# Split w_out for the second slot's second product of a linear-attention and FFN kernel

## The chip, the cores and the metric

The kernel runs on one core of one Trainium2 chip. The metric is the device time of one execution in microseconds; lower is better. Three runs of the kernel before took 598.08, 599.2 and 603.07 us (median 599.2).

## What is computed

Two steps: a causal linear attention with a complex decay per channel, and behind it a feed-forward network (FFN) whose activation is a rational function.

```python
mag = np.sqrt(a_re * a_re + a_im * a_im)
scale = np.minimum(mag, 0.999) / (mag + 1e-06)
a_re_n, a_im_n = (a_re * scale, a_im * scale)
for t in range(S):                       # S = 768; B, H, D = 4, 8, 48
    new_re = ar * S_re - ai * S_im       # ar, ai: a_re_n, a_im_n at t
    new_im = ar * S_im + ai * S_re
    S_re, S_im = (new_re + kv, new_im)   # kv: outer product of k and v at t
    y[:, :, t] = np.einsum('bhd,bhde->bhe', q[:, :, t], S_re)
...
x = y.transpose(0, 2, 1, 3).reshape(B * S, H * D)    # 3072 x 384
h = x @ w_in                                         # 384 x 2048
P = a[0] + a[1] * h + a[2] * h2 + a[3] * h3
Q = 1.0 + np.abs(b[0]) * np.abs(h) + np.abs(b[1]) * h2
g = P / (Q + 1e-06)
return g @ w_out                                     # 2048 x 384
```

q, k, v and the decays are float32; w_in and w_out come as float64.

## The kernel before

**Units and slots.** The sequence is cut into 6 chunks of 128 steps. A unit is one chunk of one batch (24 units); two units make a pair, and the kernel works through 12 pairs, its slots. For a unit, `norm` and `angle` build the decay's running product `MM` (three scans) and its running angle `T` (one scan for two units), `trig` takes sines and arc tangents on ScalarE (ACT), `outer` multiplies q and k by them into `Q`, and DMAs turn the result over into `HQ`. `attn` then does the matmuls on TensorE (PE): keys turned (L611), scores (L624), which VectorE (DVE) masks into `ST`, values (L642), and the chunk's contribution to the state `St` (L662). x of the unit is written to a ring of three.

**The FFN of a slot** is `ffn` (L678). The first four slots take one pair each, 256 tokens; after that, two pairs go together, 512 tokens. h is made 128 of its 2048 rows at a time, a block; there are 16 blocks f, and in the first four slots two blocks share a bank `ph` and make a group, 8 groups to a slot. A group goes through these steps: first product into `ph` (L701, PE); on ACT squares, an absolute value and a reciprocal square root (L366) in the buffers `Af` and `Zf`; on DVE the operations that join them to g (L351); second product (L717, PE), which adds the group's two blocks to the sums in `po0` and `po1`. The second product of a group is written behind the first product of the group two further on. There are four buffers g, three `Af`, two `Zf` and three banks `ph`.

**Split and unsplit.** Matmuls are done in one of two ways. Unsplit, both operands are float32: one matmul for each of the three 128-wide strips of the 384 columns. Split, weight and moving operand are each a high half in the type fp32r and a low half (the rest), and three matmuls high x high, low x high, high x low stand for one, nine for a block. The global `WHOLE = 2` says that slots 0 and 1 use unsplit weights, for both products; later slots use split ones. With unsplit weights ACT's second square root step lies in a PSUM bank (`po2`), and DVE has four operations for a group: `ph`, `Af<-Af,co,po`, `Af<-Af,po`, `g<-ph,co,Af`. With split weights g is made as two halves and there are five: `ph`, `g<-ph,co,Zf` (the high half), `Af<-Af,co,g`, `Af<-ph,co,Af`, and the low half `g<-Af,Zf`, which can run on DVE or GpSimd (POOL).

**Weights.** w_in and w_out arrive as raw float64 bits by DMA and are folded to float32 tiles `wi` (12 of 128 x 512) and `wo` (16 of 128 x 384) by `fold` (L431 to L449). `split` then makes the halves of all weights, with `halve`: the high half is a copy (L465 when ACT does it), the low half a subtraction (L351) on DVE or POOL. High halves of w_out are called `wh`, its low halves take the tile of a `wo` that is used up. L1041 to L1044 place all of it around the end of slot 1, in the order's time from 1.3 to 2.5 slots.

**What sets the order.** Operations are collected in a plan, each with the engines that could run it. The global `ORDER` (L235) is a recorded table: the position of each operation in the program and its engine. Instructions of one engine run in that order. DMAs are issued from SyncE (SP), save a few from ACT. `rouse` (L667, L673) adds matmuls into an unused bank (fillers, `po<-wi,ident` and `po<-Q,ident`, 128 x 256 each, two records), which the order may put on PE or drop.

## Time and profile before

| | |
|---|---|
| median of three runs | 599.2 us |
| profiled execution | 602.15 us, span 600.5 us |
| mean granted clock of TensorE | 0.973 |
| busy share of PE, DVE, ACT, POOL | 93%, 91%, 87%, 47% |
| stretch 0 to 57 us | loads, folding, the first two units |
| 57 to 112 us, 112 to 168 us | FFN of slots 0 and 1, both unsplit |
| 168 to 214 us, 214 to 270 us | FFN of slots 2 and 3, split, 256 columns |
| from 270 us on | wide FFN slots, 512 columns |

The profile is one execution, seen by the hardware profiler. The stretches are where the first products of a slot begin, within some us, since neighbouring slots overlap. A busy PE is not PE at its peak, since matmuls are pipelined and their ends are modelled. A float32 matmul that is not split shows as two records. The idle time of an instruction is what its engine idled ahead of it, with the instruction that ended the wait as the trace infers it.

### The profile page before, as it was taken

What the parts mean: (1) busy time and instruction counts of PE and PEld (TensorE: products, weight loads), DVE (VectorE), ACT (ScalarE), POOL (GpSimd) and SP (SyncE); (2) the same over time, 40 slices, a digit from 0 to 9 for tenths busy, and PEclk for the clock granted to TensorE, in tenths of its full rate; (3) what the DMA queues carried; (4) which work ended last, traced back from release to release, by engine and by line L of the source; (5) the groups of instructions that cost most, each with busy time, mean ns of one, the idle gap of its engine ahead of it and who ended that gap; (6) DMA issues with size and microseconds to landing.
All of it is one profiled execution on the core that took longest, in us unless ns stands there. A gap on an engine that the chain in (4) does not pass through costs nothing.

```text
span 600.5 us, 15652 instructions
## 1 busy us (share of the span) xinstructions
PE 558.3 (93%) x6240; PEld 470.2 (78%) x6240; DVE 543.7 (91%) x924; ACT 524.7 (87%) x872; POOL 284.3 (47%) x253
## 2 busy tenths in 40 slices
PE   0467999999999999999999999999999999999995
PEld 0356888888899998997888788878888887878884
DVE  7996999899999999999999989999898788889884
ACT  7986999999998999989999989979998796588781
POOL 4483555357554648536674753555615346000000
PEclk9766999999999999999999999999999999999998
DMA  8996466464532365546362145324053314110001
GB/s 298 292 262 213 141 139 140 116 150 96 100 107 49 79 157 130 103 119 134 90 128 71 41 117 136 101 37 137 28 121 112 47 36 100 21 52 2 0 2 58
DMA packets 39185, 64.02 MB, mean 107 GB/s; under 512 B 4416, under 2 KB 25152, under 8 KB 39104
## 3 DMA queue, kind: packets, MB, share of 16 engines
q1 hardware_dynamic: 38528, 62.28, 41.4%
q8 instruction: 51, 0.84, 0.7%
q10 hardware_dynamic: 576, 0.66, 0.5%
q14 instruction: 30, 0.25, 0.1%
HBM read 39.32 MB, written 4.72 MB: 73 GB/s over the span
## 4 chain that ended last, share of the span: by engine, by line
PE 46%; ACT 11%; DVE 8%; issue 2%; DMA 1%; SPq 0%; DVEq 0%; ACTq 0%
PE ph L701 20%; PE po L717 19%; ACT Zf L366 4%; PE at L642 4%; PE at L624 2%; DVE Af L351 2%; ACT Af L366 2%; DVE g L351 2%; DVE ph L351 2%; PE at L662 1%; ACT L366 1%; ACT SQ L366 1%; DMA QK<-in_qk 1%; DVE Q L351 1%; PE at L611 1%
## 5 line engine op out<-in xcount | busy, mean ns | idle before, releaser
L717 PE MATMUL po<-g,wh 128*128 128x512 f32 (+1 forms) x576 | 168.2, 360 | 0.0
L701 PE MATMUL ph<-X,wiH 128*128 128x512 f32 (+1 forms) x576 | 144.2, 364 | 2.9 <-DVE Af L351 2.9
L717 PE MATMUL po<-g,wo 128*128 128x256 f32 (+1 forms) x462 | 140.3, 367 | 0.0
L717 PEld LDWEIGHTS po<-g,wh 128*128 128x128 f32 x576 | 103.1, 188 | 17.9 <-issue 1.4
L701 PEld LDWEIGHTS ph<-X,wiH 128*128 128x128 f32 x576 | 96.7, 188 | 21.8 <-issue 2.8
L717 PEld LDWEIGHTS po<-g,wo 128*128 128x128 f32 x462 | 86.9, 189 | 12.2 <-DVE ph L351 0.2
L351 POOL TENSOR_TENSOR g<-Af,Zf 128x512 fp32r<-128x512 f32 x30 | 40.0, 1333 | 100.7 <-ACT Zf L366 64.1
L366 ACT ACTIVATE Zf<-Af,co 128x512 f32<-128x512 f32 x80 | 57.8, 723 | 25.2 <-DVE ph L351 24.3
L351 DVE SCALAR_TENSOR_TENSOR ph<-Zf,co,ph 128x512 f32<-128x512 f32 x96 | 71.8, 748 | 7.1 <-ACT Zf L366 5.6
L351 DVE SCALAR_TENSOR_TENSOR g<-ph,co,Zf 128x512 fp32r<-128x512 f32 x80 | 59.6, 745 | 15.8 <-ACT Zf L366 14.1
L366 ACT ACTIVATE Af<-Af,co 128x512 f32<-128x512 f32 x96 | 69.1, 721 | 0.7
L366 ACT ACTIVATE Zf<-ph,co 128x512 f32<-128x512 f32 x96 | 65.2, 680 | 4.1 <-DVE g L351 1.5
L701 PE MATMUL ph<-X,wi 128*128 128x512 f32 (+1 forms) x264 | 67.3, 358 | 0.0
L351 DVE SCALAR_TENSOR_TENSOR Af<-Af,co,g 128x512 f32<-128x512 f32 x80 | 64.3, 804 | 2.6
L366 ACT ACTIVATE Af<-ph 128x512 f32<-128x512 f32 x96 | 56.5, 588 | 9.2 <-PE ph L701 9.1
L351 DVE SCALAR_TENSOR_TENSOR Af<-ph,co,Af 128x512 f32<-128x512 f32 x80 | 59.7, 746 | 1.2
L701 PEld LDWEIGHTS ph<-X,wi 128*128 128x128 f32 x264 | 45.7, 188 | 8.1
L366 ACT ACTIVATE Zf<-Zf 128x512 f32<-128x512 f32 x80 | 50.4, 630 | 1.9
L701 PE MATMUL ph<-wh,wi 128*128 128x256 f32 x192 | 44.8, 381 | 0.0
L351 POOL TENSOR_TENSOR RU<-MM,RU 128x384 f32<-128x384 f32 x18 | 22.7, 1259 | 39.4 <-DVE RU L351 33.4
L351 DVE TENSOR_TENSOR ST<-at,cmask 128x512 f32<-128x512 f32 x48 | 31.6, 683 | 10.1 <-ACT ph L431 4.7
L701 PEld LDWEIGHTS ph<-wh,wi 128*128 128x128 f32 x192 | 36.0, 190 | 5.1 <-PE ph L701 0.2
(204 smaller groups left out, 1103.8 us busy)
## 6 DMA issues: line engine op xcount, KB each, us to landing
HQ<-Q SPq DMA_DIRECT2D x141, 128.0 KB, 4.5
AA<-in_aa SPq DMA_DIRECT2D x23, 384.0 KB, 4.0
QK<-in_qk SPq DMA_DIRECT2D x23, 384.0 KB, 4.3
V<-in_v SPq DMA_DIRECT2D x24, 320.0 KB, 4.9
g<-in_w_out SPq DMA_DIRECT2D x8, 384.0 KB, 5.7
wh<-in_w_in SPq DMA_DIRECT2D x6, 512.0 KB, 6.6
wh<-in_w_out SPq DMA_DIRECT2D x8, 384.0 KB, 4.9
g<-in_w_in SPq DMA_DIRECT2D x6, 512.0 KB, 6.9
```

The lines of the kernel that those rows point to most:

```text
L351: call = lambda e: getattr(e, kind)(*map(real, args), **{k: real(x) for k, x in kw.items()})
L366: e.activation(o(), i(), f, **kw)
L611: e.transpose(pt[:, i].bitcast(F32R), hq[:, 4 * g + i, 1, :], ident)
L624: e.matmul(pst[32 * q:32 * q + 32, i + y, s0:C], hf[:, h, 1, s0:s0 + 32], hf[:, h, 0, s0:C], start=True, stop=True)
L642: e.matmul(py[32 * y:32 * y + 32, min(j, 2), :], l, sts[h // 4][:, h % 4, :] if q is None else hf[:, h, 0, :], start=q is None and j == 0, ...
L662: e.matmul(pd[m:m + 32, h], kT[:, h, m:m + 32], V[:, n:n + D], start=True, stop=True)
L701: e.matmul(o, wt[f // 4 * NJ + j][:, f % 4 * P:f % 4 * P + P], moving(j, hl), start=n == 0, stop=n == len(prods) - 1)
L717: e.matmul(o[:, cols], wt[:, j * P:j * P + P], gg, start=(f == 0 and n == 0 and cols.start == 0), stop=(f == NFF - 1 and n == len(prods) - ...
```

## The change

The second product of slot 1 uses split w_out, where it used unsplit float32 weights. A second global, `WHOLE_OUT = 1`, says up to which slot the second product is unsplit; `ffn` takes it as `last` and uses it for the second product, for DVE's chain and for the sign of the output. The first product of slot 1 stays unsplit. So g of slot 1 is now made in two halves, by the five operations on DVE instead of the four. `split` does w_in and w_out apart, and w_out's part is placed one slot earlier (0.3 to 1.5 in place of 1.3 to 2.5). The line numbers of the changed kernel are one or two higher.

```diff
-WHOLE = 2
+WHOLE, WHOLE_OUT = 2, 1
...
 ORDER = (
-    "c-lQ!2Y8m%6@I@zJ0!U`EE#PQz)_{e5vUZEB?z(vg$gR5EKvhNnIXsq6Gen1j0izMhKwo%P-#I?P*jMvMW_`*0%5cW`EJ4pS^w#KZ>Z1z{Nww+JI;B}d){;I"
...
+    "c-lo+3!KhX{{EhK?lZ<YST@%gq!Qg#)}`9qk_g#UBA3M&*DR}u+*|kCuw;?aY{F0x8fs(9pQNnZ_8&7YNi=iL7-o!`_xV5Pj6VO*eBOC~@9%dm-^=rTp6~g^"
...
-    def split():
+    def split(i, o):
 
         for k, x in enumerate(wi):
-            wiH.append(buf(cst, [P, FW], F32R, f"wiH{k}"))
-            wiL.append(buf(cst, [P, FW], F32R, f"wi{k - 1}"))
-            halve(FW, x, lambda h=wiH[k]: h.t, wiH[k], wiL[k])
-            if k % 3 == 2:
+            if i:
+                wiH.append(buf(cst, [P, FW], F32R, f"wiH{k}"))
+                wiL.append(buf(cst, [P, FW], F32R, f"wi{k - 1}"))
+                halve(FW, x, lambda h=wiH[k]: h.t, wiH[k], wiL[k])
+            if o and k % 3 == 2:
...
-    def ffn(c, xs, b0, whole=False, end=False):
+    def ffn(c, xs, b0, whole=False, last=False, end=False):
...
-        ns = 1310 if whole else 9 * (MM512 if F == 1 else 123)
+        ns, ns2 = (1310 if x else 9 * (MM512 if F == 1 else 123) for x in (whole, last))
...
-                r = (wo[f],) if whole else ((wh[f // 3], f % 3), woL[f])
+                r = (wo[f],) if last else ((wh[f // 3], f % 3), woL[f])
...
-                    if whole:
+                    if last:
                         prods = ((wo[f], g[:, x * T:x * T + T]),)
...
-                pe(ns, run, (g, *r, *po), po)
+                pe(ns2, run, (g, *r, *po), po)
...
-            z_ = buf(ps, [P, 512], F32, "po2") if whole else b_
+            z_ = buf(ps, [P, 512], F32, "po2") if last else b_
...
-            scal(AF.Square, 512, tz, tz, (z_,), (z_,), psum=whole)
-            if whole:
+            scal(AF.Square, 512, tz, tz, (z_,), (z_,), psum=last)
+            if last:
...
-            ffn(slice(i // 2, i // 2 + 1), [(xTs[i], i % XB)], 2 * (i % 2), i < WHOLE)
+            ffn(slice(i // 2, i // 2 + 1), [(xTs[i], i % XB)], 2 * (i % 2), i < WHOLE, i < WHOLE_OUT)
...
-        if i == WHOLE - 1:
-            mark = len(plan.ops)
-            split()
-            plan.spread(mark, WHOLE - 0.7, WHOLE + 0.5)
+        for x in sorted({WHOLE, WHOLE_OUT}):
+            if i == x - 1:
+                mark = len(plan.ops)
+                split(x == WHOLE, x == WHOLE_OUT)
+                plan.spread(mark, x - 0.7, x + 0.5)
```

The table `ORDER` is replaced as a whole, so every operation may have a new place. Three places follow; numbers behind names tell buffers of one name apart. Some counts over the whole order: PE runs 31 fillers before and 34 after, of which 14 and 11 stand behind the first of slot 0's first products (in slots 0 and 1: 11 and 3 before, 3 and 8 after). Of the low halves of slot 1's eight g, DVE makes seven and POOL one. Of the 16 low halves of w_out, POOL makes 11 and DVE 5 in either order. At the end of slot 1, seven second products stand in a row on PE after the change.

First, PE in slot 1, from the middle of its early first products up to its first second product. `ph<-wh4,wi` is the first product (the x of this slot lies in `wh4`), `po1<-wi,ident` and `po1<-Q,ident` are fillers, `po0` and `po1` the second product's sums. Before:

```order
L673 MATMUL po1_1229<-wi0_191,ident_69 128x256
L701 MATMUL ph_1331<-wh4_1058,wi3_277 128x256
L701 MATMUL ph_1331<-wh4_1058,wi4_320 128x256
L701 MATMUL ph_1331<-wh4_1058,wi5_331 128x256
L701 MATMUL ph_1331<-wh4_1058,wi3_277 128x256
L701 MATMUL ph_1331<-wh4_1058,wi4_320 128x256
L701 MATMUL ph_1331<-wh4_1058,wi5_331 128x256
L717 MATMUL po0_1359<-g_1295,wo0_166 128x256 x2
L717 MATMUL po1_1362<-g_1295,wo0_166 128x256
```

After, at the same second product:

```order
L702 MATMUL ph_1324<-wh4_1043,wi7_415 128x256
L702 MATMUL ph_1324<-wh4_1043,wi8_505 128x256
L674 MATMUL po1_1329<-wi0_160,ident_69 128x256 x4
L718 MATMUL po0_1459<-g_1304,wh0_1114 128x256
L718 MATMUL po0_1459<-g_1304,wo-1_1207 128x256
L718 MATMUL po0_1459<-g_1304,wh0_1114 128x256 x2
L718 MATMUL po0_1459<-g_1304,wo-1_1207 128x256
L718 MATMUL po0_1459<-g_1304,wh0_1114 128x256
L718 MATMUL po1_1466<-g_1304,wh0_1114 128x256
L718 MATMUL po1_1466<-g_1304,wo-1_1207 128x256
L718 MATMUL po1_1466<-g_1304,wh0_1114 128x256
```

What moved: the first block's second product was three float32 matmuls and is nine matmuls of halves (`wh` the high half of w_out, `wo-1` the low one); four fillers stand ahead of it where one stood two groups earlier; and it follows the first product of an older group, since first products run ahead by fewer groups there.

Second, DVE ahead of the mask on the scores of the second unit of slot 0, before slot 0's first product. `ST<-at,cmask` is the mask (of the two halves of the heads), `ph<-ph,wh`, `wi<-wh,ph` fold a tile of w_in, `St<-St,at` adds to the state of the first unit, `SQ`, `T`, `MM` and `RU` belong to the decays of the units behind. Before:

```order
L443 SCALAR_TENSOR_TENSOR ph_452<-ph_452,wh1_450 128x512
L351 TENSOR_TENSOR St_93<-St_93,at0_111 96x4x2x48
L447 SCALAR_TENSOR_TENSOR wi8_484<-wh2_387,ph_415 128x512
L351 SCALAR_TENSOR_TENSOR MM_444<-MM_444,ncar_101,SQ_382 128x128
L447 SCALAR_TENSOR_TENSOR wi6_498<-wh1_450,ph_452 128x512
L351 SCALAR_TENSOR_TENSOR SQ_382,fl_103<-AA_353,SQ_382 128x384
L351 TENSOR_TENSOR ST_559<-at1_112,cmask_70 128x512
L351 TENSOR_TENSOR ST_568<-at0_111,cmask_70 128x512
L351 SCALAR_TENSOR_TENSOR MM_444<-MM_444,ncar_101,SQ_382 128x128 x2
L443 SCALAR_TENSOR_TENSOR ph_573<-ph_573,wh0_553 128x384
L351 SCALAR_TENSOR_TENSOR T_292<-SQ_382,T_292 128x384
```

After:

```order
L351 SCALAR_TENSOR_TENSOR SQ_351,fl_103<-AA_349,SQ_351 128x384
L351 SCALAR_TENSOR_TENSOR T_271<-SQ_351,T_271 128x384
L351 SCALAR_TENSOR_TENSOR MM_354<-MM_354,ncar_101,SQ_351 128x128
L351 SCALAR_TENSOR_TENSOR RU_308<-Z_321,RU_308 128x3x128
L351 TENSOR_TENSOR St_93<-St_93,at0_111 96x4x2x48
L443 SCALAR_TENSOR_TENSOR ph_476<-ph_476,wh2_440 128x512
L447 SCALAR_TENSOR_TENSOR wi8_505<-wh2_440,ph_476 128x512
L351 COPY ncar_101<-MM_263 128x3
L443 SCALAR_TENSOR_TENSOR ph_474<-ph_474,wh1_393 128x512
L447 SCALAR_TENSOR_TENSOR wi6_533<-wh1_393,ph_474 128x512
L351 TENSOR_TENSOR ST_552<-at0_111,cmask_70 128x512
L351 TENSOR_TENSOR ST_596<-at1_112,cmask_70 128x512
```

What moved: the first operations on `SQ`, `T` and `MM`, which stood behind the mask (`MM` x2 and `T`) or between the folds, stand ahead of it with `RU`, and two folds stand just ahead of the mask.

Third, DVE at the first groups of slot 1. `ph<-Zf,co,ph` opens a group's chain; `Q`, `QK`, `RU`, `Z`, `SQ` and `ncar` belong to the units behind. Before, a group's chain:

```order
L351 SCALAR_TENSOR_TENSOR ph_1232<-Zf_1262,co_89,ph_1232 128x512
L351 COPY ncar_101<-MM_1015 128x3
L351 SCALAR_TENSOR_TENSOR RU_1240<-Z_1252,RU_1240 128x3x128
L351 SCALAR_TENSOR_TENSOR Af_1245<-Af_1245,co_89,po2_1266 128x512
L351 SCALAR_TENSOR_TENSOR Af_1245<-Af_1245,po2_1266 128x512
L351 SCALAR_TENSOR_TENSOR g_1295<-ph_1232,co_89,Af_1245 128x512
L351 TENSOR_TENSOR QK_1259<-QK_1259,RU_1240 128x768
```

After, two groups' chains interleaved:

```order
L351 SCALAR_TENSOR_TENSOR g_1283<-ph_1247,co_89,Zf_1254 128x512
L351 SCALAR_TENSOR_TENSOR ph_1259<-Zf_1289,co_89,ph_1259 128x512
L351 SCALAR_TENSOR_TENSOR Af_1256<-Af_1256,co_89,g_1283 128x512
L351 SCALAR_TENSOR_TENSOR Af_1256<-ph_1247,co_89,Af_1256 128x512
L351 SCALAR_TENSOR_TENSOR g_1304<-ph_1259,co_89,Zf_1289 128x512
L351 SCALAR_TENSOR_TENSOR Af_1276<-Af_1276,co_89,g_1304 128x512
L351 SCALAR_TENSOR_TENSOR Af_1276<-ph_1259,co_89,Af_1276 128x512
L351 TENSOR_TENSOR Q_1317<-QK_1310,CO_1050 128x768
L351 TENSOR_TENSOR g_1304<-Af_1276,Zf_1289 128x512
L351 TENSOR_TENSOR Z_1315<-MM_945,Z_1315 128x384
L351 TENSOR_TENSOR SQ_1308<-SQ_1308 128x384
L351 TENSOR_TENSOR g_1283<-Af_1256,Zf_1254 128x512
```

What moved: a group has `g<-ph,co,Zf`, two operations on `Af` and the low half `g<-Af,Zf` in place of two operations on `Af` with `po2` and one g; the low halves are DVE's here, and the second group's chain is begun before the first one's is done.

## Rows read from the trace of the kernel before

**Rows 1.** The page's head: busy us, share of the span, instructions.

```profile
span 600.5 us, 15652 instructions
PE 558.3 (93%) x6240; PEld 470.2 (78%) x6240; DVE 543.7 (91%) x924; ACT 524.7 (87%) x872; POOL 284.3 (47%) x253
```

**Rows 2.** Windows: stretch, length; PE, PEld, DVE, ACT, POOL; clock, DMA, GB/s.

```profile
0.00:57.00 57.00, 26.27 (x292) 20.10 (x293) 47.15 (x103) 43.90 (x82) 30.91 (x45) 0.76 0.87 265
57.00:112.00 55.00, 55.00 (x567) 47.73 (x566) 53.19 (x97) 53.74 (x91) 29.00 (x32) 1.00 0.52 133
112.00:168.00 56.00, 55.55 (x589) 48.27 (x589) 53.57 (x94) 54.18 (x95) 33.15 (x29) 1.00 0.57 121
...
460.00:590.00 130.00, 130.00 (x900) 104.40 (x899) 109.65 (x178) 99.13 (x159) 29.36 (x19) 1.00 0.19 40
```

**Rows 3.** Waits of PE, 57 to 590 us: us in all, times, longest.

```profile
PE ph L701 <- DVE Af L351: 2.9, 4, 1.2
```

**Rows 4.** Timeline of PE: start, us, instructions; shapes out and in, count.

```profile
50.48 2.36 PE L624 MATMUL at<-HQ 96*32 96x96 f32 x64
...
67.16 0.88 PE L662 MATMUL at<-V,kT 128*32 128x48 f32 x48
...
72.39 0.59 PE L673 MATMUL po<-Q,ident 128*128 128x256 f32 x2
72.82 4.05 PE L717 MATMUL po<-g,wo 128*128 128x256 f32 x18
76.71 2.75 PE L701 MATMUL ph<-wh,wi 128*128 128x256 f32 x12
...
159.87 7.93 PE L717 MATMUL po<-g,wo 128*128 128x256 f32 x36
...
199.93 0.28 PE L717 MATMUL po<-g,wh 128*128 128x256 f32 x1
...
202.08 0.52 PE L701 MATMUL ph<-X,wiH 128*128 128x256 f32 x3
```

**Rows 5.** Timeline of DVE; in brackets the idle time before and its end.

```profile
51.91 0.69 DVE L351 TENSOR_TENSOR ST<-at,cmask 128x512 f32<-128x512 f32 x1 [4.70 <-ACT ph L431]
...
58.94 1.75 DVE L351 TENSOR_TENSOR_SCAN T<-smask,T 128x768 f32<-128x768 bf16 x1
60.60 0.53 DVE L449 SCALAR_TENSOR_TENSOR wo<-g,ph 128x384 uint32<-128x384 uint32 x1
...
161.39 0.74 DVE L351 SCALAR_TENSOR_TENSOR g<-ph,co,Af 128x512 f32<-128x512 f32 x1
...
263.92 0.68 DVE L351 TENSOR_TENSOR g<-Af,Zf 128x512 fp32r<-128x512 f32 x1
264.53 0.55 DVE L351 SCALAR_TENSOR_TENSOR SQ<-AA,SQ 128x384 f32<-128x384 f32 x1
```

**Rows 6.** Groups of instructions, whole span, then 57 to 168 us: busy us, mean ns.

```profile
L366 ACT ACTIVATE Zf<-Af,co 128x512 f32<-128x512 f32 x80 | 57.8, 723 | 25.2 <-DVE ph L351 24.3
L351 DVE SCALAR_TENSOR_TENSOR Af<-Af,co,g 128x512 f32<-128x512 f32 x80 | 64.3, 804 | 2.6
L366 ACT ACTIVATE Zf<-Zf 128x512 f32<-128x512 f32 x80 | 50.4, 630 | 1.9
...
L366 ACT ACTIVATE po<-Af,co 128x512 f32<-128x512 f32 x16 | 11.1, 692 | 0.1
L366 ACT ACTIVATE po<-po 128x512 f32<-128x512 f32 x16 | 9.4, 587 | 0.2
```

**Rows 7.** Tiles of w_out's halves, 60 to 260 us: count, ns min/median/max, starts.

```profile
L465 ACT ACTIVATE wh<-wo x13: 504/514/533, 106.0 to 198.4; 128x384 fp32r<-128x384 f32 x13
...
L351 POOL TENSOR_TENSOR wo<-wo,wh x10: 998/1017/2317, 150.0 to 196.5; 128x384 fp32r<-128x384 f32 x10
```

**Rows 8.** Tile g on DVE, whole span, columns as in rows 7.

```profile
L351 DVE SCALAR_TENSOR_TENSOR Af<-Af,co,g x80: 721/752/1983, 167.8 to 588.5; 128x512 f32<-128x512 f32 x80
...
L351 DVE TENSOR_TENSOR g<-Af,Zf x50: 659/689/2231, 170.5 to 590.1; 128x512 fp32r<-128x512 f32 x50
```

## Prediction: what the change does to the time

> **What bounds the kernel now.** I read the page's head first: TensorE, VectorE (DVE) and ScalarE (ACT) are busy for 93%, 91% and 87% of a span of 600.5 us [rows 1]. Busy time of pipelined matmuls says little about TensorE, so the windows by stage come next. In 57 to 112 us DVE is busy for 53.19 of 55 us and in 112 to 168 for 53.57 of 56: it is idle for 1.81 + 2.43 = 4.2 us in these two slots, and ACT for hardly more; in 460 to 590 us DVE is idle for 20 of 130 [rows 2]. The waits say who holds whom: from 57 us on, TensorE's largest wait, for first products that need DVE to free their bank, is 2.9 us in all [rows 3]. So slots 0 and 1 are bound by TensorE and DVE together, with DVE about as tight as an engine gets, and the late wide slots by TensorE alone. Before 57 us, where slot 0's first product begins, the loads and the first two units' attention set the pace; the granted clock is 0.76 on average there and 1.00 behind it [rows 2].
>
> The profiled run took 602.15 us around its span of 600.5, where the median of the runs is 599.2. What I work out in the span I add to 599.2. About 1% (6 us) is what a measurement of this kernel can tell from no change.
>
> **TensorE's sum.** An unsplit second product of one block f is three float32 matmuls, each shown as two records. Eighteen records (three blocks) run from 72.82 to 76.71: 216 ns a record, 1.297 us a block [rows 4]. A split block of 256 columns is nine records: eighteen (two blocks) run from 199.93 to 202.08, 119 ns each, 1.075 us a block [rows 4]. Slot 1 has 16 blocks, so it saves 16 x 0.222 = 3.5 us. The new order also has other fillers: behind the first product of slot 0 there are 14 now and 11 in the new order, 3 less at 0.43 us each (72.39 to 72.82 [rows 4]): 1.3 us. One unit's state matmuls (67.16, 0.88 us [rows 4]) move ahead of the first product, where TensorE waits anyway: 0.9 us. TensorE has 5.7 us less to do from the first product on. At the last blocks of slot 1 it has gained 4.9 of these; fillers in slot 1 go up from 3 to 8 while those in slot 0 go down from 11 to 3. By this alone the kernel takes 599.2 - 5.7 = 593.5 us.
>
> The Trainium skill ("FP8 and Floating Point Precision", TensorE Precision Notes) has a true FP32 product make four passes through the array. Three products of halves would then cost three quarters, and the saving would be 16 x 1.297 / 4 = 5.2 us, an estimate from that page. The trace disagrees: 1.075 / 1.297 is 0.83, and I use 3.5 us.
>
> **What DVE and ACT get in return.** For a group of two blocks the unsplit chain has four operations on DVE, the split one four of about the same length and a fifth, the low half g <- Af,Zf. The order puts seven of slot 1's eight fifths on DVE and one on POOL. One takes 0.61 us of DVE from start to start (263.92 to 264.53 [rows 5]): 7 x 0.61 = 4.3 us. ACT pays 723 + 630 ns where it paid 692 + 587 [rows 6]: 8 x 0.07 = 0.6 us. POOL is busy for 33 of 56 us in slot 1 [rows 2], so its one hides.
>
> Halving w_out costs nothing new: 16 copies and 16 subtractions, as before, with five of the subtractions on DVE in either order. It also moves less than its name says. ACT's copies began at 106.0 us already, and only the last starts at 198.4; POOL's subtractions of halves run from 150.0 to 196.5 [rows 7]. What is new is that all must be done by the end of slot 1.
>
> The rest is order. I counted DVE's instructions of either order up to the last g of slot 1 and priced each kind by its distance from start to start. The new order has 9.5 us more: the 4.3 above; 2.5 for a scan and a wrap of the next pair's angles that stood behind and now stand ahead (the scan is 1.66 of it, 58.94 to 60.60 [rows 5]); 2.7 net of small operations, the largest of them sums and products that POOL did. Up to the last g of slot 3 the same count gives +8.0, and at the end of slot 4 +5.6: much of it is work done earlier, not more work.
>
> **What absorbs it.** First, DVE waits 4.70 us ahead of the mask on unit 1's scores (51.91 [rows 5]). The row names ACT, but the scores themselves come only at 50.48 to 52.84 on TensorE [rows 4]. The new order has 2.8 us more of DVE work ahead of that mask, as the second piece of order shows, so 2.8 of the 9.5 us fill a wait. I leave the wait's end where it is: no DMA is added, the copies of unit 1's keys are issued behind two weight loads as now, about one load less stands ahead of them in all, and what moves behind them (that unit's values) is needed only after the scores. A first product that begins 2 us earlier or later moves everything by as much, and belongs to the range. Second, TensorE takes the last g of slot 1 at 159.87 + 24 x 0.216 = 165.05 (the 36 records from 159.87 on are six blocks [rows 4]), and it was ready at 161.39 + 0.74 = 162.13 [rows 5]: 2.9 us of slack. Third, DVE's own idle time of 4.2 us.
>
> So TensorE is at its last blocks of slot 1 later than now by 9.5 - 2.8 - 2.9 = 3.8 us if DVE recovers none of its idle time, and earlier by 0.4 if it recovers all. Its own lead of 4.9 us can't be used then: it waits for g. Behind this point it has 0.8 us less to do than now, so the end comes between +3.0 and -1.2. DVE's surplus does not grow after it (+8.0, then +5.6), while TensorE's waits of 2.9 us [rows 3], all behind slot 1, get shorter when TensorE comes later to them. I take the middle, +0.9, and half of these waits, -1.5, and come to -0.6: **598.5 us** as a round figure, with 594.5 to 602.5 as this case's own range. Of the 5.7 us that TensorE saves, DVE takes back nearly all.
>
> **The rivals.**
>
> (a) TensorE decides alone: DVE closes its gaps because first products lie ready, and the surplus hides. For it: TensorE's longest wait for DVE is 2.9 us in sum [rows 3]. Against it: DVE would have to work without a break through two slots in which ACT too is busy for 53.74 of 55 and 54.18 of 56 us [rows 2]. It gives 593.5.
>
> (b) Slower: DVE's new operations are blocked by POOL. Those that read two SBUF tiles, Af <- Af,co,g and g <- Af,Zf, have medians of 752 and 689 ns but maxima of 1983 and 2231 [rows 8]. Slot 1 gets 15 of them. At what the first kind's mean lies above its median (804 [rows 6] against 752) they cost 15 x 0.05 = 0.8 us; at the maxima 15 x 1.4 = 21 us. It decides from about 0.45 us each on, 6.7 us in all: 606 and more, 612 at half the maxima.
> The Trainium skill ("SBUF — State Buffer", Who interferes with whom) has a rule that speaks against this change: a DVE instruction with two SBUF inputs contends with a GpSimd one that reads SBUF, and the loser waits for all of it. By that rule and these rows it happens, and is rare here.
>
> (c) Slower: the low halves of w_out come too late. In the new order seven second products stand in a row on TensorE at the end of slot 1, 1.075 us each, and of the last twelve blocks' low halves POOL makes seven, at 1.02 us each and 2.32 at worst [rows 7]. If all seven come at the worst, TensorE waits 7 x (2.32 - 1.08) = 8.7 us: 607. It decides from the point where halves come more than 1.1 us apart. Against it: the other five are DVE's, their copies stand early in ACT's order, and POOL is idle for 23 of 56 us [rows 2].
>
> (d) No change at all: the wide slots from 270 us on are the same work for TensorE, and DVE's surplus just equals TensorE's lead. This is the middle of my forecast, 599.2.
>
> **How the numbers follow.** The forecast with (d) has 0.62, (a) 0.18, (b) 0.08, (c) 0.12. Faster by over 1% is under 593.2: half of (a) and a tail of the forecast, where the first product comes earlier, 0.14. Slower by over 1% is over 605.2: most of (b) and (c), 0.17. Within 1%: 0.69. The range, 591 to 606, takes in (a) with an earlier start and the near ends of (b) and (c); some 0.16 lie outside.
>
> **What would show it.** Right: sixteen split blocks at 1.08 us in slot 1; DVE's wait ahead of unit 1's mask down to some 2 us; DVE idle for less than 3 us from the first product to the end of slot 1; second products of slot 1 that wait for g. Wrong: waits of these for wo or wh (c); means over 1200 ns for DVE's two-tile operations (b); no wait for g at all (a); or a first product of slot 0 that begins more than 2 us away from 57.

## The result and the profile after

The changed kernel takes 607.93 us (median of four runs, 607.83 to 608.52) where the kernel before takes 599.29: a ratio of 1.0132, 95% interval 1.0094 to 1.0169. It is slower, and outside the forecast range. The profiled execution took 608.03 us around a span of 606.3. The span of before was 600.5 in an execution 2.9 us above its median, so the traces show 5.8 of the 8.6 us.

The page's head of the kernel after answers to [rows 1]:

```profile
span 606.3 us, 15765 instructions
PE 557.2 (92%) x6294; PEld 470.6 (78%) x6294; DVE 549.4 (91%) x925; ACT 527.9 (87%) x875; POOL 283.1 (47%) x255
```

The windows of the kernel after, in the columns of [rows 2]:

```profile
0.00:57.00 57.00, 25.42 (x348) 18.78 (x348) 48.73 (x104) 44.65 (x81) 28.16 (x41) 0.85 0.93 279
57.00:112.00 55.00, 52.09 (x433) 44.18 (x437) 52.20 (x98) 52.40 (x91) 31.62 (x35) 0.97 0.45 117
112.00:168.00 56.00, 50.00 (x657) 44.34 (x650) 54.09 (x87) 53.66 (x93) 24.19 (x21) 0.97 0.49 119
...
460.00:590.00 130.00, 129.90 (x897) 103.77 (x898) 107.82 (x177) 100.48 (x162) 33.48 (x25) 1.00 0.18 40
```

TensorE idles for 2.9 us of slot 0's stretch and for 6.0 of slot 1's, where it idled for 0.4 in both together [rows 2], and its mean granted clock is no longer 1.00 there. DVE is as full as before. The end of the kernel is unchanged. The largest waits of TensorE from 57 us on, where the largest of [rows 3] was 2.9 us:

```profile
PE at L612 <- DVE St L351: 3.7, 1, 3.7
PE at L643 <- issue: 2.5, 1, 2.5
PE po L718 <- DVE g L351: 2.2, 2, 1.7
PE ph L702 <- DVE Af L351: 2.1, 2, 1.7
PE ph L702 <- DVE g L351: 1.2, 1, 1.2
```

TensorE's timeline after, from slot 0's first product to the last blocks of slot 1, in the columns of [rows 4] (in brackets the idle time before and what ended it):

```profile
56.98 0.42 PE L643 MATMUL at<-ST,V 128*32 128x128 f32 x1 [2.53 <-issue]
57.33 1.22 PE L674 MATMUL po<-Q,ident 128*128 128x256 f32 x2
58.35 1.91 PE L702 MATMUL ph<-wh,wi 128*128 128x256 f32 x4
...
113.52 2.86 PE L702 MATMUL ph<-wh,wi 128*128 128x256 f32 x12
...
151.99 0.54 PE L612 MATMUL at<-ident,HQ 128*128 128x128 f32 x4 [3.67 <-DVE St L351]
...
160.65 0.39 PE L718 MATMUL po<-g,wh 128*128 128x256 f32 x1
...
168.31 0.52 PE L702 MATMUL ph<-X,wiH 128*128 128x256 f32 x3
...
173.94 0.40 PE L718 MATMUL po<-g,wh 128*128 128x256 f32 x2
...
176.10 0.28 PE L718 MATMUL po<-g,wh 128*128 128x256 f32 x1
```

Slot 1's first product in the kernel before:

```profile
112.43 3.83 PE L701 MATMUL ph<-wh,wi 128*128 128x256 f32 x17
```

Slot 0 begins at 58.35 us, 1.6 later than before, with its first records at a granted clock of 0.50 behind a stall. Slot 1, from its first first product to its last second product, lasts 62.9 us (113.5 to 176.4) where it lasted 55.4 (112.4 to 167.8). Behind slot 1 the kernel after needs 429.9 us, 2.8 less than before (432.7). With half a microsecond gained in slot 0 this is the whole: 1.6 - 0.5 + 7.5 - 2.8 = 5.8 us.

### The profile page after: what moved, and what is told of

Read it like the earlier page. It is cut to its first block, busy times and chain, and to the rows that moved or that the text cites. A ratio compares the mean times of both kernels' runs of the same rounds, so it can differ in the third digit from the quotient of the medians.

```text
span 606.3 us, 15765 instructions
## 1 busy us (share of the span) xinstructions
PE 557.2 (92%) x6294; PEld 470.6 (78%) x6294; DVE 549.4 (91%) x925; ACT 527.9 (87%) x875; POOL 283.1 (47%) x255
## 4 chain that ended last, share of the span: by engine, by line
PE 69%; DVE 7%; issue 1%; ACT 0%; DVEq 0%
PE po L718 29%; PE ph L702 28%; PE at L643 5%; PE at L625 4%; DVE Af L351 2%; PE at L663 2%; DVE g L351 1%; PE at L612 1%; DVE MM L351 1%; DVE T L351 0%; DVE Q L351 0%; DVE ph L351 0%; DVE X L351 0%; DVE St L351 0%; DVE ST L351 0%
## 5 line engine op out<-in xcount | busy, mean ns | idle before, releaser
L718 PE MATMUL po<-g,wh 128*128 128x512 f32 (+1 forms) x672 | 185.6, 350 | 0.6 <-DVE g L351 0.5
L718 PE MATMUL po<-g,wo 128*128 128x256 f32 (+1 forms) x411 | 131.8, 355 | 1.7 <-DVE g L351 1.7
L718 PEld LDWEIGHTS po<-g,wh 128*128 128x128 f32 x672 | 118.1, 189 | 19.5 <-issue 1.8
L351 POOL TENSOR_TENSOR g<-Af,Zf 128x512 fp32r<-128x512 f32 x37 | 49.1, 1328 | 96.6 <-ACT Zf L366 53.6
L718 PEld LDWEIGHTS po<-g,wo 128*128 128x128 f32 x411 | 77.4, 189 | 11.4 <-DVE g L351 2.1
L351 DVE SCALAR_TENSOR_TENSOR g<-ph,co,Zf 128x512 fp32r<-128x512 f32 x88 | 65.7, 746 | 18.2 <-ACT Zf L366 16.8
L351 DVE SCALAR_TENSOR_TENSOR Af<-Af,co,g 128x512 f32<-128x512 f32 x88 | 72.4, 823 | 2.5
L351 DVE SCALAR_TENSOR_TENSOR Af<-ph,co,Af 128x512 f32<-128x512 f32 x88 | 65.7, 747 | 1.8
L366 ACT ACTIVATE Zf<-Zf 128x512 f32<-128x512 f32 x88 | 55.4, 629 | 2.0
L351 POOL TENSOR_TENSOR SQ<-SQ 128x384 f32<-128x384 f32 x18 | 22.1, 1226 | 46.5 <-ACT SQ L366 46.5
L351 POOL TENSOR_TENSOR Q<-QK,CO 128x768 f32<-128x768 f32 x16 | 32.2, 2011 | 20.3 <-ACT CO L566 10.8
```

What stands on the lines that cost most here:

```text
L351: call = lambda e: getattr(e, kind)(*map(real, args), **{k: real(x) for k, x in kw.items()})
L366: e.activation(o(), i(), f, **kw)
L718: e.matmul(o[:, cols], wt[:, j * P:j * P + P], gg, start=(f == 0 and n == 0 and cols.start == 0), stop=(f == NFF - 1 and n == len(prods) - ...
```

## The experiments

One table first. Ratios are against runs of before that were made together with each kernel (medians of 598.8 to 601.2). "Slot 1" is the duration just defined, read from TensorE's timeline of each profiled execution; it leaves out the start, which scatters: slot 0's first product came at 49.8 to 56.7 us in profiles of kernels that begin as before does. Each duration is from a single execution. One run of `low_half_on_pool` took 3050 us, which nothing here explains; it is left out of its row. The four kernels whose names begin with halves or all, and those without the low half or the halving, leave out work or operands that the result needs, so they are tests and no candidates.

| kernel | median us | ratio, 95% interval | slot 1 us |
|---|---|---|---|
| before | 599.3 | 1 | 55.4 |
| after | 607.9 | 1.0132, 1.0094 to 1.0169 | 62.9 |
| dve_early | 612.6 | 1.0215, 1.0155 to 1.0275 | 59.8 |
| dve_late | 605.8 | 1.0100, 1.0067 to 1.0133 | 54.9 |
| x1_old_order | 626.6 | 1.0443, 1.0381 to 1.0504 | 79.7 |
| x2_new_order_unsplit | 617.4 | 1.0289, 1.0227 to 1.0350 | 69.7 |
| states_later | 605.9 | 1.0092, 1.0056 to 1.0127 | 63.0 |
| before_states_early | 599.7 | 0.9979, 0.9950 to 1.0008 | 55.0 |
| stalls_out | 604.9 | 1.0070, 1.0039 to 1.0101 | 64.1 |
| no_low_half | 607.5 | 1.0094, 1.0058 to 1.0131 | 63.7 |
| low_half_on_pool | 614.2 | 1.0251, 1.0182 to 1.0320 | 69.0 |
| state_early | 608.2 | 1.0137, 1.0086 to 1.0188 | 64.0 |
| copies_on_pool | 608.1 | 1.0120, 1.0050 to 1.0190 | 63.9 |
| fillers_out | 606.8 | 1.0135, 1.0077 to 1.0193 | 63.5 |
| halves_free | 611.2 | 1.0153, 1.0064 to 1.0243 | 66.5 |
| halves_free_no_low | 609.1 | 1.0124, 1.0042 to 1.0205 | 61.2 |
| all_three_relieved | 608.8 | 1.0124, 1.0066 to 1.0182 | 62.6 |
| all_four_relieved | 604.8 | 1.0116, 1.0055 to 1.0177 | 57.6 |
| no_halving_before | 601.9 | 1.0013, 0.9981 to 1.0045 | 55.0 |
| no_halving_after | 608.0 | 1.0119, 1.0082 to 1.0157 | 62.3 |

**What DVE's time is worth.** Two kernels add some 10.5 us of DVE work to the kernel before and nothing else. `twice` makes the helper issue the instruction two times.

```diff
-                stt(lambda g=g: g.t, tp, c0, ta, (a_, ph, "co"), (g,))
+                stt(lambda g=g: g.t, tp, c0, ta, (a_, ph, "co"), (g,), twice=True)
```

> The kernel before, with the last operation of g's chain (g<-ph,co,Af) run twice in each of the 16 groups of slots 0 and 1: the same values are written twice, TensorE's work and the order are unchanged. 16 x 0.67 = 10.7 us more on DVE. Theory D: DVE has no more than its 4.2 us of idle time to hide it, and g has 2.9 us of slack at the end of slot 1: 3.6 to 7.8 us later there, less some 1.5 us of TensorE's later waits: 602 to 606. Rival P (TensorE sets the pace, g lies ready): 599.3 to 600.

```diff
-                stt(lambda g=g: g[:, 0], tp, c0, tz, (ph, z_, "co"), ((g, 0),))
+                stt(lambda g=g: g[:, 0], tp, c0, tz, (ph, z_, "co"), ((g, 0),), twice=c.start >= 4 and k % 2 == 0)
```

> The control to the run with twice-written g in slots 0 and 1: the kernel before, with g<-ph,co,Zf run twice in every second group of the last two wide FFN slots (from some 430 us on), 16 x 0.65 = 10.4 us more on DVE. Theory D: DVE is idle for 20 of 130 us there and TensorE alone sets the pace: 599 to 600.5. If DVE time costs its length anywhere in this kernel: 606 to 610.

The early work costs 12.9 us (9.3 to 16.5) for 10.7: about its full length, and no sign that idle time or slack hides any of it. The theory that DVE's time decides (D in the texts on record) named the place rightly and was too low. The late work, 10.4 us, costs 6.0 us (4.0 to 8.0), some six tenths: neither the nothing that D gave it nor the full length. TensorE's waits in that run, 460 to 590 us, where the kernel before has none:

```profile
PE ph L701 <- DVE Af L351: 4.3, 6, 1.5
```

DVE is idle there for 17 of 130 us (113.30 busy in that window) and TensorE waits for it all the same. DVE's own longest wait in that window says where its idle time lies:

```profile
DVE g L351 <- ACT Zf L366: 9.5, 10, 1.5
```

It stands ahead of g, the doubled operation, where DVE waits for ACT; what is added behind that wait delays the rest of the group, and with it the bank `ph`. So idle time of DVE covers 4.4 of 10.4 us in the late slots and nothing that can be told in the early ones.

**The order and the work apart.** Two kernels cross them; only the table differs from the kernel whose work they do (of `x1_old_order` after, of `x2_new_order_unsplit` before).

```diff
 ORDER = (
-    "c-lo+3!KhX{{EhK?lZ<YST@%gq!Qg#)}`9qk_g#...
+    "c-lQ!33yaRwm#KKy3-*^RTAK__>vG@K8AS+0*Zhl...
```

> The changed kernel's work (slot 1's second product split, w_out halved a slot earlier) in the order of before: every operation that both kernels have keeps its place and its engine of before, slot 1's g is made by the five operations in the places of the four, and w_out's halves stand some 24 to 34 places ahead of the products that use them. Theory D (DVE sets the pace in slots 0 and 1, and the new order loads it with more than the split product does): DVE has 7 low halves more, 4.3 us, 2.9 us of it hidden by the slack that g has before slot 1's last products; at most 1.4 us of blocked operations come on top: 599.3 + 1.4 to 2.8, so about 601, 599 to 604 with what the late Zf buffers cost. Theory S (the split product itself is what costs: a longer chain that holds its Zf buffer to the end): 606 to 608, as the changed kernel.

```diff
 ORDER = (
-    "c-lQ!2Y8m%6@I@zJ0!U`EE#PQz)_{e5vUZEB?z...
+    "c-lo+2Y8i5);{08DK`mW1|o=okc6VEU}4u?c_?...
```

> The work of before (both products of slot 1 unsplit) in the order of the changed kernel: operations that both have stand where the change put them, slot 1's g has its four operations again, and w_out's halves are made where before made them, behind slot 1. Theory D: the changed kernel's 607.9 less seven low halves on DVE (4.3 us) and less the 1.4 us by which Af<-Af,co,g ran longer than its median: about 602, 601 to 604. Theory S: 599 to 600. If the late begin of slot 0's first product (58.35 us in the changed kernel, 56.70 before) comes from the order, it is seen here too and makes up 1.7 us of the difference.

Both are slower than either kernel, 626.6 and 617.4, and far outside all that was expected, so they can't share the loss out. Operations that only one of the kernels has were put where the author chose. Windows of 112 to 168 us, first of `x1_old_order`, then of `x2_new_order_unsplit`:

```profile
112.00:168.00 56.00, 44.79 (x541) 38.83 (x539) 48.06 (x73) 40.28 (x73) 30.13 (x22) 0.91 0.48 93
```

```profile
112.00:168.00 56.00, 47.60 (x574) 40.01 (x568) 47.01 (x76) 48.14 (x81) 17.37 (x19) 0.94 0.45 106
```

TensorE, DVE and ACT all have more idle time than in before or after. A likely reading, which no run tests by itself: each of the four engines runs a fixed list, and work that doesn't fit its list blocks what is queued behind it. The split product in the old order costs some 26 us against before, the unsplit one in the new order 9.5 more than the split one. Each of these two orders serves its own work better.

**The start.** TensorE stood still for 2.53 us among 32 records of value matmuls that wait for nothing in the trace (the row at 56.98 us above). ACT's and DVE's lists stood behind it:

```profile
51.95 1.34 DVE L351 TENSOR_TENSOR ST<-at,cmask 128x512 f32<-128x512 f32 x2 [1.73 <-PE at L625]
...
58.37 0.36 DVE L438 TENSOR_SCALAR wh<-wh 128x384 f32<-128x384 f32 x1 [2.59 <-ACT ph L431]
```

```diff
 L625 MATMUL at_112<-HQ_96 32x32 x2
-L663 MATMUL at_111<-V,kT 32x48 x24
 L643 MATMUL at_112<-ST,V 32x128 x16
...
 L702 MATMUL ph<-wh_511,wi_379 128x256
+L663 MATMUL at_111<-V,kT 32x48 x24
```

> The changed kernel with the state matmuls of slot 0's second unit (48 small matmuls) behind three groups of first products again, as in the kernel before, and the sum into its state behind the first g. In the changed kernel TensorE stood still for 2.53 us among that unit's value matmuls, at 54.4 to 57.0 us, without a wait that the trace shows, while 16 KB of its instructions came in at 54.6 to 55.6; ACT and DVE stood behind it, DVE for 2.59 us. Theory I (it ran out of instructions because 144 small matmuls stand in a row): no such stall, slot 0's first product some 2 us earlier, DVE's wait gone: 605.5 to 606.5. If the stall has to do with something else: 607.5 to 608.5, with the stall in its trace.

605.9, as theory I (TensorE runs out of instructions among many small matmuls) has it; the stall is gone and slot 0's first product comes at 53.3 us. The gain by the ratio, 1.0092 against 1.0132, is within both intervals:

```profile
51.65 1.08 PE L643 MATMUL at<-ST,V 128*32 128x128 f32 x32 [0.91 <-DVE ST L351]
52.66 0.70 PE L674 MATMUL po<-Q,ident 128*128 128x256 f32 x2
53.34 0.92 PE L702 MATMUL ph<-wh,wi 128*128 128x256 f32 x3
```

The same move made in the kernel before (there L662 ahead of L642):

> The kernel before with one group of matmuls moved: the 48 state matmuls of slot 0's second unit stand ahead of its values, as the new order has them, and nothing else changes its place. Theory I (with score, state and value matmuls in a row TensorE uses up its instructions faster than they come): a stall of 2 to 2.8 us in that unit's values, slot 0's first product 1.5 to 2.5 us later against runs of before, 601.5 to 603.5 where before has some 600.7 in the same call, though 0.9 us of TensorE's work moves out of slot 0. If the stall belongs to the rest of the new order: 599.5 to 601.

599.7, no slower, and no stall in its trace, so the small matmuls in a row don't bring it by themselves. In the profiles of kernels that begin in the new order the stall is there in 11 of 12, with 0.3 to 3.2 us, and in none of the eight that begin otherwise. But the rest of theory I, that TensorE waits for instructions, is borne out by the DMA records. In all eleven TensorE stops behind the same record, the 31st of these 32, and goes on 1.3 to 1.6 us after a block of 16 KB of instructions has landed. In the kernel after this block is under way from 54.64 to 55.58 us and TensorE goes on at 56.98; the DMA view of 54 to 56 us has it as the only one:

```profile
q8 instruction: 1, 0.02, 2.9%
```

In the twelfth kernel, `low_half_on_pool`, the block had landed 1.6 us before TensorE came to that record, and in `before_states_early` 2.6 us before. So the stall is most likely a wait for instructions at a place that the program fixes. Why the block comes too late in this order is open.

```diff
+L351 TENSOR_TENSOR St<-St,at_111 96x4x2x48
 L351 SCALAR_TENSOR_TENSOR g<-ph,co,Zf 128x512
...
 L351 SCALAR_TENSOR_TENSOR Af<-Af,co,g 128x512
-L351 TENSOR_TENSOR St<-St,at_111 96x4x2x48
```

> The changed kernel with one operation of DVE moved: the sum into the state St of slot 1's first unit stands four operations earlier, ahead of g<-ph,co,Zf, T and two scans of MM, so that TensorE's key transposes, which waited 3.67 us for it at 152 us, can start some 4 us earlier. Rival Q: 3 to 4 us less, 604 to 605. Theory D: DVE's work up to the last g is the same, so the wait only moves: 607 to 608.5.

No gain: the 3.67 us went over into other waits, the longest of them 2.4 us for ACT's copy of the keys. Theory Q on record, by which TensorE's stalls set the time, asked for 604 to 605 here; that speaks against it. With both moves together:

> The changed kernel with both moves together: the state matmuls of slot 0's second unit behind three groups of first products (605.9 by itself) and the sum into St ahead of the scans of MM in slot 1 (no gain by itself). Theory B: the second move has nothing to give as long as DVE's last g and the backlog hold slot 1: 605 to 606.5. If the two waits added up only while slot 0 began late: 603 to 604.5.

604.9, the best of the versions that do all of the split product's work (what is left is 0.7%, interval 0.4 to 1.0). There is no sign that the second move adds to the first: slot 1 takes 64.1 us where the first move alone has 63.0.

**One engine relieved at a time.** Each kernel takes from one engine what the new order gave it in slot 1.

```diff
-                mul(512, lambda g=g: g[:, 1], ta, tz, (a_, z_), ((g, 1),), ALU.mult, EN["glo"])
+                if not whole:
+                    mul(512, lambda g=g: g[:, 1], ta, tz, (a_, z_), ((g, 1),), ALU.mult, EN["glo"])
```

> The changed kernel without the low half of g in slot 1: the eight operations g<-Af,Zf of that slot (seven on DVE, one on POOL) are left out, and the third matmul of each split product multiplies the high half of g instead, so that TensorE's work is unchanged; all else keeps its place. What is left out: the low half of g in slot 1, so the output of that slot is less exact. Theory D (DVE sets the pace up to some 330 us, and the fifth operation is what it lacks time for): 607.9 - 7 x 0.61 = 603.6, within 602.5 to 605. Rival Q (the new order's stalls of TensorE, 3.7 us for the state and 2.5 us ahead of slot 0, set the time): 606.5 to 608.

607.5. DVE's last g comes 3.4 us earlier (170.3 against 173.7 us), and TensorE still ends slot 1 at 176.7, since it comes late itself. It waits at the same place as long as before:

```profile
152.14 0.54 PE L612 MATMUL at<-ident,HQ 128*128 128x128 f32 x4 [3.63 <-DVE St L351]
```

So the fifth operation is not what costs the time by itself; theory D, DVE's time alone, falls as a full account. (Theory Q's range takes in the 607.5, but the gain that Q asks for in `state_early` did not come.) The low halves on POOL, in the diff by a row each:

```diff
-L351 DVE TENSOR_TENSOR g<-Af,Zf
+L351 POOL TENSOR_TENSOR g<-Af,Zf
```

> The changed kernel with all eight low halves of g of slot 1 on POOL, in their places of the order. DVE has 4.3 us less to do, POOL 7 x 1.3 = 9.3 us more in a slot in which it is busy for 24 of 56 us. Theory D: 603.6, plus what DVE loses where POOL's new operations block its two-tile ones: 604 to 606. Rival Q: 607 to 608. If blocking by POOL gives all back: 608 to 610.

614.2, worse than leaving them on DVE and than anything expected (604 to 610): the chain that ends last in slot 1 then runs over POOL's g and `wo`. The copies of w_out on POOL, and slot 1 without fillers:

```diff
-L465 ACT ACTIVATE wh<-wo
+L462 POOL CAST wh<-wo
```

> The changed kernel with the 16 copies that make w_out's high halves on POOL instead of ACT (15) and DVE (1), in their places of the order: ACT has 15 x 0.42 = 6.3 us less to do, most of it in slot 1, and POOL some 8 us more in a time in which it is idle for half. Theory T (three engines are full in slot 1 of the new order, ACT with the copies that had been spread over slots 1 to 2.5, DVE with the low halves, TensorE with its backlog, and relieving one lets the next one show): 0 to 2 us less, 606 to 608. Theory A (ACT alone is what is left, since neither DVE's relief nor the backlog's gave anything): 602 to 604.5.

```diff
-L674 MATMUL po1_1329<-wi0_160,ident_69 128x256 x4
```

> The changed kernel without the eight fillers of slot 1 (8 x 0.43 = 3.4 us of TensorE, all between 124 and 135 us, ahead of the first split second product). Theory T (several chains end together): TensorE gets to the second unit's key transposes 3 us earlier and waits longer there for the sum into St, so 0 to 1 us less, 606.5 to 608.5, or a little more if the longer wait lowers the clock again. Theory P (TensorE's own work decides slot 1, fillers with it): 3.4 us less, 604 to 605.

608.1 and 606.8: neither is told from no change. Freeing the second products from the late halves, and letting them stand behind their g:

```diff
-                r = (wo[f],) if last else ((wh[f // 3], f % 3), woL[f])
+                z = 0 if whole and not last else f
+                r = (wo[f],) if last else ((wh[z // 3], z % 3), woL[z])
```

> The changed kernel with slot 1's second products freed from the late halves of w_out: all 16 blocks multiply the halves of block 0 (so slot 1's output is not what it should be; the halving of all of w_out goes on unchanged in its places), and the blocks 4 to 15 stand right behind their g in TensorE's order instead of in a row behind 160 us. Seen so far: the changed kernel's TensorE works without a break from 152 to 176 us, 14 of the 16 blocks in it, and takes the last g 0.4 us after DVE has it. Theory B (two chains end together: TensorE's backlog and DVE's last g): 0.4 to 1 us less, 606.5 to 608. Theory L (the late halves and the backlog they force decide alone): 4 to 6 us less, 602 to 604.

611.2, no gain, where 602 to 604 was asked for if the late halves decide alone; TensorE's waits for g rose to 7.2 us.

**Several relieved together.** These combine the edits above.

> Both relieved: slot 1's second products freed from the late halves and placed behind their g, and the low half of g in slot 1 left out (its third matmul takes the high half again; slot 1's output is wrong in both ways, TensorE's number of matmuls is the same). Theory B: now DVE's last g comes some 3.4 us earlier, as without the low half alone, and TensorE is there to take it: 3 to 4.5 us less than the changed kernel, 603 to 605, where each relief by itself gives 1 us or less. Theory L: no more than with the halves freed alone. If a third thing holds slot 1 (the keys, scores and sums of the attention): 606 to 608.

> The kernel that has slot 1's second products freed from the late halves and no low half of g in slot 1 (609.1), with the 16 copies of w_out on POOL besides. Slot 1's output is wrong in the same way as there. Its chain from 152 to 176 us ran over ACT without a break. Theory T: with the third engine relieved too the slot gets shorter: 4 to 7 us less than 609.1, 602 to 605. If something else holds slot 1 (the order itself, attention's own chain): 607 to 609.5.

> The kernel with DVE, ACT and the late halves relieved (608.8), without the eight fillers of slot 1. Its chain ran over TensorE without a break from 123 to 151.5 us, and all eight fillers, 3.4 us, lay in it. Slot 1's output is wrong as there. Theory T: now the fillers are on the path, 2.5 to 3.5 us less than 608.8: 605 to 606.5. If the slot is held by attention's transfers and sums of the next units: 608 to 609.5.

609.1 and 608.8: two and three reliefs gave nothing in the time, against the theories that let a relief of DVE and of the late halves together bring it back. The chain of waits of `all_three_relieved` (start us, us, what) names the piece that was left:

```profile
122.15 0.76 DVE Af L351
...
123.05 1.53 PE ph L702 x6
124.58 0.43 PE po L674 x2
...
127.26 0.86 PE po L674 x4
...
130.12 0.63 PE po L674 x2
...
132.94 1.73 PE po L674 x8
134.66 4.30 PE po L719 x36
```

TensorE works without a break from 123 to 151.5 us, and the eight fillers (L674) are 3.65 us of it. Without them slot 1 takes 57.6 us in place of 62.6, and the whole kernel 604.8. By ratios the two can't be told apart (1.0116 and 1.0124, against different runs of before); the gain shows in the durations of slot 1 alone, one execution each. Nor are all 5.0 us the fillers'. The windows of slot 1 in `all_three_relieved` and `all_four_relieved`, in this order:

```profile
113.28:175.89 62.61, 58.20 (x648) 52.44 (x649) 58.10 (x92) 54.66 (x91) 37.31 (x37) 0.95 0.49 112
```

```profile
111.78:169.38 57.60, 52.22 (x632) 47.01 (x633) 55.79 (x88) 53.83 (x89) 34.69 (x35) 1.00 0.54 121
```

The first ran at a mean granted clock of 0.95, the second at 1.00, and so did slot 1 of `halves_free_no_low`. Against that one's 61.2 us slot 1 is 3.6 us shorter with all four, as long as the fillers; the copies on POOL show no gain of their own.

**Is the earlier halving to blame?** Both kernels without the halving of w_out's blocks 3 to 15, all else in its place.

```diff
-                    halve(DM, wo[f], lambda f=f: wh[f // 3][:, f % 3], (wh[f // 3], f % 3), woL[f])
+                    if f < 3:
+                        halve(DM, wo[f], lambda f=f: wh[f // 3][:, f % 3], (wh[f // 3], f % 3), woL[f])
```

> The kernel before without the halving of w_out's blocks 3 to 15: 13 copies and 13 subtractions are left out, and the second products of split slots take the halves of the blocks 0 to 2 over again (their output is wrong, TensorE's work the same); every other operation keeps its place. The halving stood between 106 and 198 us there. Theory T: the removed work was spread over slots that TensorE fills, so 0.5 to 3 us less than before: 598 to 600.5 against runs of before of some 601.

> The changed kernel without the halving of w_out's blocks 3 to 15, in the same way and with every other operation in its place of the new order. ACT has some 5.5 us less, POOL and DVE 13 subtractions. Theory T: that the halving has to be done by the end of slot 1, where all engines are full, is the larger part of the loss: 4 to 6 us less than the changed kernel, 602 to 604, more than the same edit gives in the kernel before. Rival O (the order as such costs the time, whatever the halving does): 606 to 608, and the two edits give the same.

601.9 and 608.0: nothing in either kernel. The claim that the forced halving is the larger part of the loss (theory T) falls; its rival O, by which it is worth nothing, holds.

## Why the prediction was wrong

**TensorE's sum was right, and of no use.** Seven split blocks run from 160.65 to 168.31 us, 1.09 us each, against 1.075 by [rows 4]. To an unsplit block's 1.297 that is 0.84. The Trainium skill ("FP8 and Floating Point Precision", TensorE Precision Notes) states four passes for a true FP32 product; three quarters, the estimate that the prediction took from it and did not use, is not what this trace shows.

**DVE's count was right to within a microsecond.** From the mask (51.9 us in both) to the last g it takes 11.5 us longer (172.98 + 0.69 against 161.39 + 0.74). The 9.5 - 2.8 = 6.7 us of work that the forecast put behind the mask are in it, and the wait ahead of the mask fell from 4.70 to 1.73 as forecast. DVE's timeline after, the last g of slot 1:

```profile
172.98 0.69 DVE L351 TENSOR_TENSOR g<-Af,Zf 128x512 fp32r<-128x512 f32 x1
```

**The step that failed is "What absorbs it".** It let TensorE come to slot 1's end later by 3.8 us, or earlier by 0.4 if DVE recovers its idle time, took the middle, and had no term for blocked operations (it put 0.8 us of them into rival (b)). Two things happened instead. DVE recovered nothing: between mask and last g it idles for 6.1 us, 1.9 more than before, 2.59 of it behind TensorE's stall at 54 us. And DVE is busy for 2.9 us more than before beyond the 6.7 counted. That figure is a remainder: by each kind's median length, operations that run long make 2.1 us of it, nearly all in the two rows below, and some 0.8 us is work that the count missed. Those two of the kernel after, with their partners on POOL:

```profile
132.46 1.55 DVE L351 SCALAR_TENSOR_TENSOR Af<-Af,co,g 128x512 f32<-128x512 f32 x1
...
148.42 2.40 DVE L351 TENSOR_TENSOR_SCAN MM<-MM,ncar,SQ 128x128 f32<-128x128 f32 x2
```

```profile
132.46 1.00 POOL L351 TENSOR_TENSOR RU<-MM,RU 128x384 f32<-128x384 f32 x1
...
148.31 1.86 POOL L351 TENSOR_TENSOR QK<-QK,RU 128x768 f32<-128x768 f32 x1 [0.48 <-DMA QK<-in_qk]
```

`Af<-Af,co,g` has a median of 752 ns [rows 8] and takes 1.55 us. In `no_low_half` the lists stand differently at the second place: the two scans are free and take 0.85 us in place of 2.40, and `Af<-Af,co,g` meets `QK<-QK,RU` instead:

```profile
148.62 0.85 DVE L351 TENSOR_TENSOR_SCAN MM<-MM,ncar,SQ 128x128 f32<-128x128 f32 x2
149.39 2.23 DVE L351 SCALAR_TENSOR_TENSOR Af<-Af,co,g 128x512 f32<-128x512 f32 x1
```

```profile
149.09 1.98 POOL L351 TENSOR_TENSOR QK<-QK,RU 128x768 f32<-128x768 f32 x1 [1.44 <-DMA QK<-in_qk]
```

In all three places DVE's delay is what was left of POOL's operation, less 0.2 us: 0.80 of 1.00, 1.55 of 1.75 and 1.48 of 1.68. The Trainium skill ("SBUF — State Buffer", Who interferes with whom) has the loser of such a pair wait for all of the other's operation; these three agree. So the blocking was real, at some 2.1 us, under the 6.7 from which rival (b) decides; of the operations that (b) lists only one was blocked in slot 1, for 0.8 us, and the scans were not on its list. Nor do its two prices go together: 612 at half the maxima, 10.5 us, doesn't follow if 6.7 us give 606; it would be 610. With both terms the forecast's own sum comes to 3.8 + 1.9 + 2.9 = 8.6 us at the end of slot 1, where the trace has 176.4 - 167.8 = 8.6. As 2.9 is itself a remainder, this says only that the last g came 11.5 us later and that the slack of 2.9 was used up.

**Behind slot 1** the forecast gave back 0.8 + 1.5 = 2.3 us; the traces have 2.8.

**But the last g did not set the end.** The sum ends at the last g, "it waits for g", and that path was wrong. The chain that ended last in the kernel after (start us, us, what):

```profile
148.42 2.40 DVE MM L351 x2
150.83 0.64 DVE Af L351
151.47 0.47 DVE St L351
...
151.99 0.54 PE at L612 x4
...
160.72 7.75 PE po L718 x63
...
173.08 3.31 PE po L718 x27
```

It runs over DVE, the blocked scans in it, to the sum into the state `St`. TensorE had waited 3.67 us for that, with second products of 12 of the 16 blocks still ahead (`halves_free` was built on a count of 14), and then worked from 151.99 to 176.39 us without a break. The last g, at 173.67, is not on this chain; TensorE takes it 0.4 us later (174.06) as it comes by. So TensorE's lead was lost in 6.0 us of idle time before 152, and its own backlog set the end. That is why taking 3.4 us from DVE moved the last g and not the end: in `no_low_half` TensorE waits for `St` until 152.14 all the same. Two lists, TensorE's and DVE's, end within a microsecond, and no single relief gave the time back; with four together slot 1 falls to 57.6 us, 5.3 of the 7.5 us lost, some of it the clock's. How the loss divides among the lists is argued and not shown, and what remains is open.

**Rivals.** (a) fell: DVE's time costs about its full length in slots 0 and 1. (b) was real and too small; no run takes POOL's blocking away, so what it costs in the end is not measured. (c) fell: no wait of slot 1's second products for `wo` or `wh`, and freeing them gave nothing. The late wide slots are not TensorE's alone either, as `dve_late` shows.

**Fillers.** The five more in slot 1 were counted as TensorE's work and then left, as TensorE would wait for g anyway; `fillers_out` shows no gain without them. A sentence ahead of the prediction, behind the first piece of the order, is mistaken: first products run ahead by five groups in the new order where it was four, and the filler before stood one group ahead.

**Open** is why the instructions come late at 54 us in that order, and whether an order exists in which the split product pays: no other order was fitted to it, and `all_four_relieved` leaves work out and is still 1.2% above before, with the stall (2.5 us) in it. No version beat the kernel before.

## What to carry to other kernels

Idle time of an engine inside a dependent chain is little cover: here added work cost from six tenths of its length, where DVE was idle for 15%, to all of it, so ask for the idle piece by name before subtracting it. Ask also which wait ends last before the backlog begins, and not only when the last input is ready. Where a whole order was fitted to its work, a change of either is a change of all lists; here the cost could not be divided among its parts, so test reliefs together before naming a cause. A saving on an engine that is idle for under 1% gave nothing here, where the engines that feed it got more to do.

## What the runs showed of the hardware

A wait of TensorE can cost more than its length: behind the 3.67 us in which it waited for St it ran four microseconds at a mean granted clock of 0.57, so most of them at the lower level, 1.2 GHz. By an estimate from this row that is 4.00 x 0.43, some 1.7 us of work lost. The windows around it in the kernel after:

```profile
148.00:152.00 4.00, 0.33 (x6) 0.19 (x4) 4.00 (x7) 3.44 (x8) 1.86 (x1) 1.00 0.01 4
152.00:156.00 4.00, 4.00 (x71) 3.69 (x72) 4.00 (x9) 3.41 (x7) 0.74 (x1) 0.57 0.17 47
156.00:160.00 4.00, 4.00 (x85) 3.46 (x87) 4.00 (x8) 3.98 (x7) 2.64 (x3) 1.00 0.15 55
```

The 2.53 us stall was followed by the lower level too, at a granted clock of 0.50:

```profile
57.00:60.00 3.00, 3.00 (x7) 2.24 (x8) 1.63 (x3) 2.56 (x6) 0.83 (x1) 0.50 0.47 187
```

What such a wait is worth to the kernel is another matter: with the wait for St moved away (`state_early`) the time was the same.

TensorE stood still for up to 3.2 us inside one unit's matmuls without a wait in the trace, in 11 of 12 profiles of one order always behind the same record, and went on 1.3 to 1.6 us after a block of 16 KB of instructions had landed; where the block was there earlier, it did not stop.

An operation of DVE that met one of POOL's was delayed by what was left of POOL's, less 0.2 us, in the three places looked at (0.80, 1.55 and 1.48 us).

And the load phase scatters by 7 us between profiles (slot 0's first product at 49.8 to 56.7 us in kernels that begin alike), while the end of slot 0 scatters less: 107.6 to 110.3 in five of six such profiles, and 114.4 in the sixth (`no_halving_before`).
